# Attention rounds whose scores are formed two units ahead, with the probabilities turned before them

## The chip, the cores and the metric

The kernel runs on one core of a Trainium2 chip. The metric is the device time of one execution in microseconds (us), taken as the median of several runs.

## The reference

Two computations follow one another. Attention over 4 batches of 8 heads, 768 positions and a head size of 64, in which a position sees the 128 positions up to itself and the first four positions ("sinks"), gives a matrix x of 3072 rows and 512 columns. A mixture of eight experts is then applied to x, with gates that are normalized eight times by rows and by columns.

```python
scores = scale * np.matmul(q, k.transpose(0, 1, 3, 2))
keep = is_sink | in_window            # pos < 4, or 0 <= rel < 128
scores = np.where(keep, scores, -1e9)
a = np.exp(scores - np.max(scores, axis=-1, keepdims=True))
a = a / (np.sum(a, axis=-1, keepdims=True) + 1e-09)
x = np.matmul(a, v)                   # turned to 3072 x 512
...
P = np.exp(x @ w_gate - max)          # 8 normalizations by rows and columns
for e in range(8):
    out += P[:, e:e+1] * (np.maximum(x @ w1[e], 0) @ w2[e])
```

## The kernel before

The attention is cut into 48 units, numbered n: a unit is one batch, one block i (0 to 5) of 128 positions and one half of the heads (four heads). For a unit the kernel turns queries and keys (`transpose_qk`, L484 on VectorE or L489 on TensorE), forms the scores of its four heads against up to 260 keys (`scores`, L512), takes each head's maximum on VectorE while it adds the mask (`soften`, L520) and the exponentials with their sums on ScalarE (L523), divides (`divide`: VectorE adds 1e-9 and takes the reciprocal, L529 and L530, and GpSimd scales, L532), turns the probabilities (`transpose_halves`, L569: 16 matmuls of 64 rows each into two banks, which VectorE and ScalarE copy to PT, L571), turns the sinks' probabilities, which GpSimd has gathered into SS (L581, L582), into PS (`transpose_sinks`, L587 and the ScalarE copy L589), and multiplies by the values (`values`, L624). `store_x` takes the result to xr (L641 on ScalarE, L637 on VectorE).

These steps are spread over rounds. In round n before the change stand the scores, maxima, exponentials and division of unit n+1, the turning of unit n and the values of unit n-1. From round 6 on (the steady rounds) the order on every engine is the order in which the code is written, so each engine takes its instructions strictly in that order and waits where one isn't ready. Rounds up to 5 (`early_round`) are ordered by hand on TensorE alone.

TensorE is never left without work: `run_fill` adds to each round a piece of the first expert, which needs one of two things: twelve matmuls into the bank f (L732), whose result ScalarE takes with a relu (L737) and VectorE takes again with a list called `late` (L738), or six matmuls (L748), whose result is added up from a list called `mid` (L756 on VectorE) or on ScalarE. There is one bank f, so a piece waits until the reading of the piece before is over. `late` stands behind the second head's maximum, `mid` behind the last. In some rounds, two blocks at a time, the gates' logits are formed (`run_gates`, L672) in the bank of head 2's scores, and ScalarE copies them (L675); their second transposition (L680) comes in the midst of the fill. Such gate rounds are 9, 15, 19, 23, 27, 31, 35, 39 and 43 (and 47).

PSUM has eight banks here: f, t0 and t1 for turned probabilities, O for the values, and st0 to st3 for the scores of the four heads. Before the change st0 also takes the sinks' transposition of a round. At the end of a round ScalarE has its relu and the casts of weights (L708) or of x (L657) for the experts behind the attention, and GpSimd the subtractions that belong to them (L658, L709).

Behind the attention (from about 225 us) come the gates' normalization and the experts.

Of the kernel before, what the change touches and what calls it, by code (L numbers as in the profile page):

```python
# [11 lines left out]
F32R = mybir.dt.float32r  # L12
# [222 lines left out]
def tile_sink_attention_moe(ctx: ExitStack, tc: tile.TileContext, q, k, v, wg, w1, w2, out):  # L235
# [27 lines left out]
    def f32(ap):  # L263
        return ap.bitcast(F32)
# [105 lines left out]
    def st_tile(shape, k=None):  # L370
        if k is None:
            k, turns[0] = turns[0] % 4, turns[0] + 1
        return ps_st.tile(shape, F32, name=f"st{k}")
# [34 lines left out]
    def flush(todo):  # L408
        for f in todo[:]:
            f()  # L410
        todo.clear()
# [56 lines left out]
                              (k, q)[a][b, h, s * GB * P:(s + 1) * GB * P, c * SQ:(c + 1) * SQ].rearrange("(g t) d -> t g d", t=SQ))  # L468

    def squares_due(n):  # L470
        G, r = divmod(n + 8, 2 * GB)
        if FIRST <= G < 2 * B:
            load_squares(G, PARTS[6 * r:6 * r + 6])

    def transpose_qk(n):

        b, i, hh = units[n]
        us[n] = {}
        h0 = hh * HH
        t = KQ[hh]  # L480
        to = t[:, :, SINK:].rearrange("p r (a c) -> p r a c", a=2)[:, :, :, turn_of(b, i)]
        if n >= 2 * GB * FIRST:
            src = KS[n // (2 * GB)].rearrange("p (r a i t) -> p r a i t", r=HP, a=2, i=GB)[:, hh * NP:(hh + 1) * NP, :, i % GB]
            us[n]["high"] = nc.vector.transpose(to, src).ins  # L484
        else:
            pt = bank2([P, 4, P]) if 2 < n < STEADY + 2 else st_tile([P, 4, P], {0: 0, 1: 3, 2: 0}.get(n, 1))
            for pr in range(NP):
                for j, nm in enumerate(("kr", "qr")):
                    nc.tensor.transpose(pt[:, 2 * pr + j, :], raws[nm, b, i][:, h0 + 2 * pr:h0 + 2 * pr + 2, :].rearrange("p h d -> p (h d)"), ident)  # L489
                    if n < 2 and (pr, j) in ((0, 0), (1, 1)) and (n, pr) != (0, 1):  # L490
                        spin(1, 5 - 2 * pr)
            us[n]["high"] = nc.scalar.copy(to, pt.rearrange("p (r a) t -> p r a t", a=2)).ins
        if i == 1:
            with nullcontext() if steady[0] else tc.issue_after(us[n]["high"]):
                (nc.scalar.copy if steady[0] else nc.vector.tensor_copy)(t[:, :, 0:SINK], t[:, :, place(b, 0)][:, :, 0:SINK])

    def scores(n, pr):

        b, i, hh = units[n]
        u = us[n]  # L500
        K, Q = KQ[hh][:, :, seen(b, i)], KQ[hh][:, :, CW:][:, :, turn_of(b, i)]
        if pr == 0:
            u["sc"] = att.tile([P, HH, CW], F32, name="sc", bufs=3)
            u["st"] = att.tile([P, 3, HH], F32, name="st", bufs=3)
            u["ps"] = {}
        hs = range(2 * pr, 2 * pr + 2)
        ps = {h: st_tile([P, K.shape[2]], h) for h in hs}
        u["ps"].update(ps)

        for h in hs:  # L510
            r0 = (h % 2) * D
            nc.tensor.matmul(ps[h], lhsT=Q[r0:r0 + D, pr, :], rhs=K[r0:r0 + D, pr, :], start=True, stop=True)  # L512

    def soften(n, hs):

        b, i, hh = units[n]
        sc, st, ps = (us[n][x] for x in ("sc", "st", "ps"))
        sc = sc[:, :, seen(b, i)]
        for h in hs:
            us[n]["maxed"] = nc.vector.tensor_tensor_reduce(out=sc[:, h, :], in0=ps[h], in1=masks[place(b, i).start, min(i, 2)][:, seen(b, i)], op0=ALU.add, op1=ALU.min,  # L520
                                           scale=-scale, scalar=3.0e38, accum_out=st[:, 0, h:h + 1]).ins
        for h in hs:
            nc.scalar.activation(sc[:, h, :], sc[:, h, :], AF.Exp, bias=st[:, 0, h:h + 1], scale=-1.0, accum_out=st[:, 1, h:h + 1])  # L523
# [36 lines left out]
    def transpose_halves(n):  # L560

        b, i, hh = units[n]
        sc = us[n]["sc"]
        ws = sorted([(spot(n, 0), 1)] + ([(spot(n - 2, 1), 0)] if i else []))
        ts = [pst.tile([P, len(ws), HH, D], F32, name=f"t{r}") for r in range(2)]
        for h in range(HH):
            for j, (_, w) in enumerate(ws):
                for t, rows in zip(ts, HALF):
                    nc.tensor.transpose(t[:, j, h, :], sc[rows, h, place(b, i + 1 - w)], ident[rows, rows])  # L569
        PT = spots(PTR[hh], [p_ for p_, _ in ws]).rearrange("p h s t -> p s h t")  # L570
        return [lambda: nc.vector.tensor_copy(PT[:, :, :, HALF[0]], ts[0]), lambda: nc.scalar.copy(PT[:, :, :, HALF[1]], ts[1])]  # L571
# [11 lines left out]

    def transpose_sinks(n):

        tsk = st_tile([SK, P], 0 if steady[0] else 3)
        nc.tensor.transpose(tsk, f32(SS[units[n][2]]), ident)  # L587
        PS = us[n]["PS"] = att.tile([SK, P], F32R, name="PS", bufs=4)
        nc.scalar.copy(PS, tsk)  # L589

    def due_keys(n):

# [341 lines left out]
    def steady_round(n):  # L934

        if n % 2 == 0:
            if on(n):
                load_rows(("vr",), n // 2)
            if on(n + 2) and units[n + 2][1] == 0:
                load_sinks(units[n + 2][0])  # L940
        if n in ROWS:
            ROWS[n][0](ROWS[n][1])
        squares_due(n)
        if on(n + 1):
            for pr in range(NP):
                scores(n + 1, pr)
        ending = n >= L - 1
        if ending:
            flush(late)
            flush(mid)  # L950
        if ending:
            run_fill(2)
        lows = transpose_halves(n) if on(n) and not ending else []
        turned = n + 2 < 2 * GB * FIRST
        if on(n + 2) and not turned:
            transpose_qk(n + 2)
        if on(n + 1):
            for h in range(HH):
                soften(n + 1, (h,))
                if h == 1:  # L960
                    flush(late)
        flush(late)
        flush(mid)
        if on(n - 1):
            values(n - 1)
        run_gates(2)
        if on(n + 1):
            for pr in range(NP):
                divide(n + 1, range(2 * pr, 2 * pr + 2))
            if units[n + 1][1]:  # L970
                gather_sinks(n + 1)
        if n == L - 1:
            lows = transpose_halves(n)
        flush(lows)
        flush(coming)
        if on(n) and units[n][1]:
            transpose_sinks(n)
        if turned:
            transpose_qk(n + 2)
        if on(n - 1):  # L980
            store_x(n - 1)
        if n == L:
            gates.extend(later)
            later.clear()
            run_gates(1, True)
        run_fill(1)
        if START + 4 < n < L:
            flush(turned_back)
        run_fill(1)
        flush(turned_back)  # L990
        if n in PIECES:
            in_turn(*plain_tiles(*PIECES[n]), nc.gpsimd if n > 2 * NB else nc.vector)
        if n == L - 8:
            first_pieces.extend(pieces1(0))
        if n == L - 2:
            first_pieces.extend(pieces1(1))
        for _ in range({L - 8: 1, L - 6: 1, L - 4: 1, L - 3: 1, L - 2: 1, L - 1: 1, L: 2}.get(n, 0)):
            in_turn(*first_pieces.pop(0))
        flush(act_end)
        if on(n):  # L1000
            b, i, hh = units[n]
            if (i, hh) == (0, 0):
                spread_sinks(b)
            elif (i, hh) == (0, 1):
                split_sinks(b)
            elif (i, hh) == (1, 0) and b:
                split_sinks_low(b)
        flush(pool_end)
        if L - 10 <= n < L - 2:
            sums1((n - (L - 10)) // 4, (n - (L - 10)) % 4)  # L1010
# [7 lines left out]
            early_round(n)  # L1018
    steady[0] = True
    with tc.manual_schedule():  # L1020
        if units[STEADY][1]:
            gather_sinks(STEADY)
        for n in range(STEADY, L + 1):
            gates += later
            later.clear()
            if n == L - 1:
                bank1 = lambda shape: st_tile(shape, 2 + next(turn[0]) % 2)
                bank2 = lambda shape: st_tile(shape, 1) if next(turn[1]) % 2 == 0 else psf.tile(shape, F32, name="f")
            steady_round(n)
        assert not gates and not later  # L1030
        for todo in (late, mid, coming):
            flush(todo)
        flush(act_end)
        flush(pool_end)
# [241 lines left out]
    def bank2(shape):  # L1276
        tails.append(tails.pop(0))
        return tails[-1][0].tile(shape, F32, name=tails[-1][1])
# [757 lines left out]
```

## Time and profile before

| | |
|---|---|
| runs | 2049.91 us median of 3 (2049.74 to 2049.99) |
| the profiled execution: its own time | 2048.75 us |
| its span, first to last instruction | 2047.0 us |
| granted TensorE clock | 0.999 of full speed |
| TensorE busy | 2030.2 us, 99% of the span |
| VectorE, ScalarE, GpSimd busy | 1500.4, 1330.4, 168.7 us |
| chain that ended last | TensorE 94%, VectorE 2%, ScalarE 2% |

The table is to be read with care: 99% is a mean over 2047 us, of which the rounds that the change touches are the stretch from 34 to 232 us. What the change is worth is read there.

### The profile page before, as it was taken

The page shows a single profiled execution, that of the slowest core. Times are in us where ns is not written, and L with a number is a line of the kernel's source. Part 1 is how long each engine was busy: PE and PEld are TensorE (multiplying, and loading weights), DVE is VectorE, ACT ScalarE, POOL GpSimd, SP SyncE. Part 2 cuts the span into 40 slices and gives each one's busy share as a digit, 9 for nine tenths or more (in the row PEclk, how much of TensorE's full clock was granted, in tenths as well). Part 3 has the DMA queues.
Part 4 walks back from the last instruction along what each step waited for, and adds up shares of the span by engine and source line. Part 5 has one row for each costly group of instructions (what it writes and reads, how often), then busy time and mean ns, then how long its engine had stood idle before and what let it go on. Part 6 is the DMA issues. An engine that isn't in the chain of part 4 may idle for free.

```text
span 2047.0 us, 30434 instructions
## 1 busy us (share of the span) xinstructions
PE 2030.2 (99%) x10305; PEld 1661.1 (81%) x10305; DVE 1500.4 (73%) x2998; ACT 1330.4 (65%) x2727; POOL 168.7 (8%) x397
## 2 busy tenths in 40 slices
PE   9999999999999999999999999999999999999998
PEld 7777877888888888888888888888888888888886
DVE  6888769999999998756668965656655655555556
ACT  7877445778778876465667766656555556556555
POOL 7766400000000000000000000000000000000000
PEclk9999999999999999999999999999999999999999
DMA  8766238778788778777776677767666666666663
GB/s 169 159 120 121 79 108 317 264 279 289 250 293 298 254 261 335 252 225 221 231 236 235 227 248 231 226 207 271 201 203 196 212 196 197 206 196 203 205 190 101
DMA packets 316547, 445.87 MB, mean 218 GB/s; under 512 B 132384, under 2 KB 203488, under 8 KB 314592
## 3 DMA queue, kind: packets, MB, share of 16 engines
q1 hardware_dynamic: 314408, 442.64, 67.9%
q8 instruction: 84, 1.38, 0.3%
q10 hardware_dynamic: 1976, 1.20, 0.2%
q14 instruction: 79, 0.65, 0.1%
HBM read 296.86 MB, written 146.90 MB: 217 GB/s over the span
## 4 chain that ended last, share of the span: by engine, by line
PE 94%; DVE 2%; ACT 2%; issue 1%; DMA 0%; POOL 0%; SPq 0%; DVEq 0%; POOLq 0%; ACTq 0%
PE c L1052 42%; PE o L1766 29%; PE held L1766 12%; PE O L624 2%; PE st L512 2%; PE f L748 1%; PE f L732 1%; ACT sc L523 1%; PE t L569 1%; PE st L732 1%; PE held L1189 0%; POOL sc L532 0%; PE o L1862 0%; DVE acc L1795 0%; PE o L1189 0%
## 5 line engine op out<-in xcount | busy, mean ns | idle before, releaser
L1777 ACT COPY acc<-o 128x512 f32<-128x512 f32 x415 | 243.4, 587 | 404.7 <-PE o L1766 403.8
L1766 PE MATMUL o<-hf,T 128*128 128x512 f32 x1620 | 404.8, 390 | 0.2 <-ACT acc L1780 0.2
L1766 PEld LDWEIGHTS o<-hf,T 128*128 128x128 f32 x1620 | 303.4, 188 | 64.7 <-ACT o L1425 1.5
L1766 PE MATMUL o<-hf,B 128*128 128x512 f32 x1080 | 274.2, 389 | 0.0
L1052 PE MATMUL c<-B,W1a 128*128 128x512 f32 x1068 | 272.2, 390 | 0.4
L1052 PE MATMUL c<-T,W1c 128*128 128x512 f32 x1068 | 256.6, 389 | 0.0
L1425 ACT COPY o<-acc 128x512 f32<-128x512 f32 x416 | 245.8, 591 | 13.0
L1766 PEld LDWEIGHTS o<-hf,B 128*128 128x128 f32 x1080 | 202.5, 188 | 42.0
L1052 PEld LDWEIGHTS c<-B,W1a 128*128 128x128 f32 x1068 | 199.5, 188 | 44.4 <-DVE A12r L1668 2.5
L1052 PEld LDWEIGHTS c<-T,W1c 128*128 128x128 f32 x1068 | 200.5, 188 | 41.7
L1668 DVE SCALAR_TENSOR_TENSOR A11r<-c,PB 128x512 f32<-128x512 f32 x90 | 62.1, 690 | 117.7 <-PE c L1052 116.5
L1672 DVE TENSOR_TENSOR A22r<-c,M 128x512 f32<-128x512 f32 x90 | 62.1, 690 | 115.5 <-PE c L1052 93.7
L1766 PE MATMUL held<-hf,T 128*128 128x512 f32 x540 | 137.1, 389 | 0.0
L1766 PE MATMUL held<-hf,B 128*128 128x512 f32 x540 | 137.0, 390 | 0.0
L1052 PE MATMUL c<-T,W1d 128*128 128x512 f32 x534 | 135.9, 389 | 0.2 <-DVE W1d L1473 0.2
L1052 PE MATMUL c<-T,W1b 128*128 128x512 f32 x534 | 135.7, 389 | 0.0
L1052 PE MATMUL c<-B,W1d 128*128 128x512 f32 x534 | 135.7, 389 | 0.0
L1473 DVE TENSOR_TENSOR hf<-S2r,hf 128x512 fp32r<-128x512 f32 x180 | 119.9, 685 | 3.3 <-ACT hf L1470 3.3
L1766 PEld LDWEIGHTS held<-hf,T 128*128 128x128 f32 x540 | 101.3, 188 | 21.1
L1766 PEld LDWEIGHTS held<-hf,B 128*128 128x128 f32 x540 | 101.1, 188 | 20.8
L1052 PEld LDWEIGHTS c<-T,W1d 128*128 128x128 f32 x534 | 100.1, 188 | 21.3 <-DVE W1d L1473 0.6
L1052 PEld LDWEIGHTS c<-T,W1b 128*128 128x128 f32 x534 | 100.1, 188 | 20.7
(273 smaller groups left out, 3276.5 us busy)
## 6 DMA issues: line engine op xcount, KB each, us to landing
T<-w2s SPq DMA_DIRECT2D x108, 512.0 KB, 4.4
r<-in_moe_w_dram SPq DMA_DIRECT2D x75, 512.0 KB, 6.1
w2s<-T SPq DMA_DIRECT2D x64, 512.0 KB, 3.2
W1a<-w1s SPq DMA_DIRECT2D x56, 512.0 KB, 3.9
W1c<-w1s SPq DMA_DIRECT2D x56, 512.0 KB, 3.7
W1d<-w1s SPq DMA_DIRECT2D x56, 512.0 KB, 3.6
B<-w2s SPq DMA_DIRECT2D x54, 512.0 KB, 4.2
w2s<-B SPq DMA_DIRECT2D x32, 512.0 KB, 4.2
```

Of the source, the lines that this page charges most:

```text
L512: nc.tensor.matmul(ps[h], lhsT=Q[r0:r0 + D, pr, :], rhs=K[r0:r0 + D, pr, :], start=True, stop=True)
L523: nc.scalar.activation(sc[:, h, :], sc[:, h, :], AF.Exp, bias=st[:, 0, h:h + 1], scale=-1.0, accum_out=st[:, 1, h:h + 1])
L569: nc.tensor.transpose(t[:, j, h, :], sc[rows, h, place(b, i + 1 - w)], ident[rows, rows])
L624: nc.tensor.matmul(o_, lhsT=x_, rhs=y_, start=(j < 2), stop=(j >= len(ops) - 2), skip_group_check=True)
L732: nc.tensor.matmul(ps, lhsT=WP[0, u][:, a, kc, c * P:(c + 1) * P], rhs=xchunk(g, w, kc, th), start=(i == 0), stop=(i == 3 * KC - 1))
L1052: nc.tensor.matmul(ps, lhsT=w1(a, k), rhs=x[:, b, k, :], start=(start and j == 0), stop=(stop and j == len(TERMS) - 1), skip_group_check=n ...
L1425: nc.scalar.copy(t, sums[order_of(g)[j]])
L1473: nc.vector.tensor_sub(made_["d"][:, 1], made_["s"], f32(made_["d"][:, 0]))
L1668: return nc.vector.scalar_tensor_tensor(RAW[q, fm], src, 0.0, PBS[part, e, th], op0=ALU.max, op1=ALU.mult)
L1672: nc.vector.tensor_add(w, T[c], T[name])
L1766: nc.tensor.matmul(o, lhsT=W2V[w2_of(q), W2_OF[m]][:, a, k * P:(k + 1) * P], rhs=F[q, H_OF[m]][:, w, :], start=(i == 0 and not late and (b ...
L1777: nc.scalar.copy(sums[m, k], o)
```

## The change

In a steady round n the scores, maxima and exponentials are now those of unit n+2. The division of unit n+1, whose exponentials were made in the round before, stands whole (four heads wide, where it was two pairs) at the round's head. On TensorE the turning of unit n comes first, and the scores behind it. The sinks' probabilities are turned in two halves of 64 rows (`sink_halves`), each into columns 260 to 323 of a bank that the scores of heads 0 and 1 of unit n+2 then fill up to column 259; ScalarE copies each half to PS. The copies of the turned probabilities and of the sinks' halves are written ahead of the maxima. On VectorE the turning of queries and keys, now of unit n+3, comes behind the maxima. Ahead of round 6 the scores, maxima and exponentials of unit 7 and the turning of unit 8 are added, once.

```diff
     def squares_due(n):
-        G, r = divmod(n + 8, 2 * GB)
+        G, r = divmod(n + 9, 2 * GB)
...
-            pt = bank2([P, 4, P]) if 2 < n < STEADY + 2 else st_tile([P, 4, P], {0: 0, 1: 3, 2: 0}.get(n, 1))
+            pt = bank2([P, 4, P]) if 2 < n < STEADY + 3 else st_tile([P, 4, P], {0: 0, 1: 3, 2: 0}.get(n, 1))
...
+    def score_tiles(n, pr):
+
+        us[n].setdefault("banks", {}).update({h: st_tile([P, DM], h) for h in range(2 * pr, 2 * pr + 2)})
...
-        ps = {h: st_tile([P, K.shape[2]], h) for h in hs}
+        ps = {h: u["banks"][h][:, 0:K.shape[2]] for h in hs}
...
+    def sink_halves(n):
+
+        banks = us[n + 2]["banks"] if on(n + 2) else {h: st_tile([P, DM], h) for h in range(2)}
+        ts = [banks[r][0:SK, CW:CW + D] for r in range(2)]
+        for t, rows in zip(ts, HALF):
+            nc.tensor.transpose(t, f32(SS[units[n][2]])[rows, :], ident[rows, rows])
+        PS = us[n]["PS"] = att.tile([SK, P], F32R, name="PS", bufs=4)
+        return [lambda t=t, rows=rows: nc.scalar.copy(PS[:, rows], t) for t, rows in zip(ts, HALF)]
...
         if on(n + 1):
+            divide(n + 1, range(HH))
+        turn_out = transpose_halves(n) if on(n) else []
+        if on(n + 2):
+            score_tiles(n + 2, 0)
+        if on(n) and units[n][1]:
+            turn_out += sink_halves(n)
+        if on(n + 2):
             for pr in range(NP):
-                scores(n + 1, pr)
-        ending = n >= L - 1
-        if ending:
+                scores(n + 2, pr)
+        flush(turn_out)
+        if n >= L - 1:
             flush(late)
             flush(mid)
-        if ending:
             run_fill(2)
-        lows = transpose_halves(n) if on(n) and not ending else []
-        turned = n + 2 < 2 * GB * FIRST
-        if on(n + 2) and not turned:
-            transpose_qk(n + 2)
-        if on(n + 1):
+        turned = n + 3 < 2 * GB * FIRST
+        if on(n + 2):
             for h in range(HH):
-                soften(n + 1, (h,))
+                soften(n + 2, (h,))
                 if h == 1:
                     flush(late)
+        if on(n + 3) and not turned:
+            transpose_qk(n + 3)
         flush(late)
         flush(mid)
         if on(n - 1):
             values(n - 1)
         run_gates(2)
-        if on(n + 1):
-            for pr in range(NP):
-                divide(n + 1, range(2 * pr, 2 * pr + 2))
-            if units[n + 1][1]:
-                gather_sinks(n + 1)
-        if n == L - 1:
-            lows = transpose_halves(n)
-        flush(lows)
         flush(coming)
-        if on(n) and units[n][1]:
-            transpose_sinks(n)
+        if on(n + 1) and units[n + 1][1]:
+            gather_sinks(n + 1)
         if turned:
-            transpose_qk(n + 2)
+            transpose_qk(n + 3)
...
     with tc.manual_schedule():
+        n = STEADY + 1
+        for pr in range(NP):
+            scores(n, pr)
+        transpose_qk(n + 1)
+        for h in range(HH):
+            soften(n, (h,))
```

The lines move by 15 or fewer: L512 becomes L518, L520 L526, L569 L575, L571 L577, L624 L639, L672 L687, L732 L747, L738 L753, L748 L763. The two new ones are L602 (a sink half's transposition) and L604 (its copy).

TensorE, round 27 before (a gate round), from the last of its 16 transpositions on; the four L512 rows stood ahead of these 16, and st with a number is one of the banks st0 to st3:

```order
L512 MATMUL st_2509<-KQ_180 128x260
L512 MATMUL st_2510<-KQ_180 128x260
L512 MATMUL st_2513<-KQ_180 128x260
L512 MATMUL st_2514<-KQ_180 128x260
L569 MATMUL t_2517<-ident,sc 128x64
L569 MATMUL t_2518<-ident,sc 128x64
...
L624 MATMUL O<-PT_188,vr 64x256 x4
L672 MATMUL st_2550<-xr,wg_raw 32x128 x8
L587 MATMUL st_2574<-ident,SS_178 96x128
L748 MATMUL f<-W1f,h_1727 128x512 x3
L680 MATMUL st_2586<-ident,part 128x128 x2
```

TensorE, the same round now:

```order
L575 MATMUL t_2515<-ident,sc 128x64
L602 MATMUL st_2532<-ident,SS_178 96x64
L602 MATMUL st_2533<-ident,SS_178 96x64
L518 MATMUL st_2532<-KQ_184 128x260
L518 MATMUL st_2533<-KQ_184 128x260
L518 MATMUL st_2541<-KQ_184 128x260
L518 MATMUL st_2542<-KQ_184 128x260
L639 MATMUL O<-PT_188,vr 64x256 x4
L687 MATMUL st_2564<-xr,wg_raw 32x128 x8
L763 MATMUL f<-W1f,h_1738 128x512 x3
L695 MATMUL st_2586<-ident,part 128x128 x2
```

The transpositions have moved ahead of the scores, and the sinks' halves stand between them and write into the buffers (2532, 2533) that the scores of heads 0 and 1 write next; the whole transposition L587 behind the gates is gone.

VectorE in that round before, each with the engines whose semaphores it waits for, from the maxima to the first pair of the division:

```order
L520 ISA sc,st<-st_2509,mask_96 128x260 [waits PE_49,Pool_49]
L520 ISA st 128x1
L520 ISA sc,st<-st_2510,mask_96 128x260 [waits PE_49]
L520 ISA st 128x1
L738 SCALAR_TENSOR_TENSOR h_2401<-f,h_2401 128x256 [waits Activation_49]
L520 ISA sc,st<-st_2513,mask_96 128x260 [waits PE_49]
L520 ISA st 128x1
L520 ISA sc,st<-st_2514,mask_96 128x260 [waits PE_49]
L520 ISA st 128x1
L529 TENSOR_SCALAR st<-st 128x2 [waits Activation_49]
L530 RECIPROCAL st<-st 128x2 [waits DVE_49]
```

VectorE in that round now:

```order
L535 TENSOR_SCALAR st<-st 128x4 [waits Activation_49]
L536 RECIPROCAL st<-st 128x4 [waits DVE_49]
L577 COPY PT_189<-t_2514 128x2x4x64 [waits PE_49]
L526 ISA sc,st<-st_2532,mask_96 128x260 [waits Activation_49,Pool_49]
L526 ISA st 128x1
L526 ISA sc,st<-st_2533,mask_96 128x260 [waits Activation_49]
L526 ISA st 128x1
L753 SCALAR_TENSOR_TENSOR h_2402<-f,h_2402 128x256
L526 ISA sc,st<-st_2541,mask_96 128x260 [waits PE_49]
L526 ISA st 128x1
L526 ISA sc,st<-st_2542,mask_96 128x260 [waits PE_49]
```

The division and the copy to PT have moved ahead of the maxima; the maxima of heads 0 and 1 (buffers 2532 and 2533) now wait for ScalarE, where they waited for TensorE.

ScalarE in that round before, from the relu of the round before on, and now:

```order
L737 ACTIVATE h_2401<-f 128x256
L523 ACTIVATE sc,st<-sc,st 128x260 x4
L675 COPY part<-st_2550 128x256
L571 COPY PT_189<-t_2518 128x2x4x64
L589 CAST PS<-st_2574 96x128
L641 COPY xr<-O 128x256 x2
```

```order
L752 ACTIVATE h_2402<-f 128x256
L577 COPY PT_189<-t_2515 128x2x4x64
L604 CAST PS<-st_2532 96x64
L604 CAST PS<-st_2533 96x64
L529 ACTIVATE sc,st<-sc,st 128x260 x4
L690 COPY part<-st_2564 128x256
L656 COPY xr<-O 128x256 x2
```

The copies to PT and PS, now three where they were two, have moved from behind the four exponentials to ahead of them, and read the two buffers that VectorE's first maxima read.

## Rows read from the trace of the kernel before

**Rows 1.** Busy time of each engine over rounds 7 to 45, with clock and DMA share.
```profile
39.36:218.81 179.45, 177.17 (x1850) 135.39 (x1850) 148.41 (x612) 140.18 (x499) 123.06 (x291) 1.00 0.64 129
```

**Rows 2.** Timeline of TensorE in round 20: start, duration, instructions.
```profile
101.48 1.15 PE L512 MATMUL st<-KQ 64*128 64x260 f32 x8
102.46 0.67 PE L569 MATMUL t<-ident,sc 64*128 64x64 f32 x16
103.06 1.08 PE L624 MATMUL O<-PT,vr 128*64 128x256 f32 x8
104.07 0.44 PE L624 MATMUL O<-PS,VS 96*128 96x128 f32 x2
104.35 0.28 PE L587 MATMUL st<-ident,SS 128*96 128x128 f32 x1
104.38 1.65 PE L748 MATMUL f<-W2f,h 128*128 128x512 f32 x6
...
105.97 0.49 PE L512 MATMUL st<-KQ 64*128 64x260 f32 x2
```

**Rows 3.** Waits of TensorE's weight loads in rounds 7 to 45: total, times, longest.
```profile
PEld st L672 <- DVE st L520: 3.8, 9, 0.5
PEld st L512 <- ACT PS L589: 3.6, 9, 0.6
...
PEld st L512 <- ACT xr L641: 2.2, 6, 0.4
...
PEld t L569 <- POOL sc L532: 0.9, 3, 0.4
```

**Rows 4.** Timeline of TensorE in round 27, a gate round.
```profile
131.79 1.15 PE L512 MATMUL st<-KQ 64*128 64x260 f32 x8 [0.36 <-ACT PS L589]
...
134.45 0.65 PE L672 MATMUL st<-xr,wg_raw 128*32 128x128 f32 x16
```

**Rows 5.** Timeline of VectorE there: `late`, head 2's maximum, its accumulator's reading.
```profile
133.63 0.42 DVE L738 SCALAR_TENSOR_TENSOR h<-f,h 128x256 fp32r<-128x256 f32 x1
133.97 0.42 DVE L520 CUSTOM_DVE_ANT_0 sc<-st,mask 128x260 f32<-128x260 f32 x1
134.32 0.08 DVE L520 DVE_READ_ACCUMULATOR2_ANT st<- 128x1 f32 x1
```

**Rows 6.** Timeline of TensorE and ScalarE in round 47, where both were free.
```profile
227.32 0.71 PE L569 MATMUL t<-ident,sc 64*128 64x64 f32 x16
...
228.16 0.59 ACT L571 COPY PT<-t 128x512 f32<-128x512 f32 x1 [0.92 <-PE t L569]
228.64 0.27 ACT L589 CAST PS<-st 96x128 fp32r<-96x128 f32 x1
```

**Rows 7.** Timeline of ScalarE behind round 18's end.
```profile
96.31 0.38 ACT L737 ACTIVATE h<-f 128x256 fp32r<-128x256 f32 x1 [0.19 <-PE f L732]
96.59 0.70 ACT L657 CAST B<-xr 128x256 fp32r<-128x256 f32 x2
97.19 0.62 ACT L708 CAST W2f<-r 128x512 fp32r<-128x512 f32 x1
97.72 0.51 ACT L523 ACTIVATE sc<-sc,st 128x260 f32<-128x260 f32 x1
```

**Rows 8.** Timeline of TensorE and ScalarE in round 6.
```profile
34.55 1.38 PE L512 MATMUL st<-KQ 64*128 64x260 f32 x7
...
37.32 0.60 PE L489 MATMUL st<-ident,kq 128*128 128x128 f32 x4
...
38.72 0.58 ACT L492 COPY KQ<-st 128x512 f32<-128x512 f32 x1
```

**Rows 9.** Timeline of VectorE in round 45: the `mid` addition.
```profile
216.44 0.69 DVE L756 TENSOR_TENSOR acc<-f,acc 128x512 f32<-128x512 f32 x1
```

**Rows 10.** Timeline of TensorE in round 26: its start and its fill.
```profile
127.27 1.15 PE L512 MATMUL st<-KQ 64*128 64x260 f32 x8
...
129.75 0.48 PE L732 MATMUL f<-B,W 128*128 128x256 f32 x2
```

**Rows 11.** Timeline of GpSimd behind round 18's end.
```profile
98.74 1.27 POOL L709 TENSOR_TENSOR W2f<-r,W2f 128x512 fp32r<-128x512 f32 x1
```

More of the change, by code (lines that the diff above doesn't have):

```diff
@@ L500, in scores @@
         u = us[n]
+        if 2 * pr not in u.get("banks", {}):
+            score_tiles(n, pr)
         K, Q = KQ[hh][:, :, seen(b, i)], KQ[hh][:, :, CW:][:, :, turn_of(b, i)]
@@ L584, in transpose_sinks @@
     def transpose_sinks(n):
-        tsk = st_tile([SK, P], 0 if steady[0] else 3)
+        tsk = st_tile([SK, P], 3)
         nc.tensor.transpose(tsk, f32(SS[units[n][2]]), ident)
```

## The prediction

> **What bounds the kernel now.** I began with the rounds as a whole. Over rounds 7 to 45 TensorE is busy for 177.17 of 179.45 us at a full clock, while VectorE has 148.41, ScalarE 140.18 and GpSimd 123.06, and the DMA engines are busy 0.64 of the time [rows 1]. So TensorE sets the pace, and no wait of it is longer than a fraction of a microsecond. Then I read one round without a wait on TensorE's timeline: scores 0.98 us from start to start, the 16 transpositions 0.60, values 1.01 and 0.28, the sinks' transposition 0.03, fill 1.59, and the next round 4.49 behind the first [rows 2]. Such a round is nothing but TensorE's own instructions. Last I read what its weight loads wait for: scores for ScalarE's copies 3.6 and 2.2 us, transpositions for GpSimd's scaling 0.9, and the gates' logits for head 2's maximum 3.8 [rows 3]. The first three can vanish with this change. The fourth is the one to watch: in round 27 head 2's accumulator is read until 134.40 [rows 5] and the logits start at 134.45 [rows 4], so in a gate round VectorE's maxima already end just in time.
>
> **What the change takes away.** The three waits sum to 6.7 us by the weight loader's rows [rows 3], but a weight load may wait beneath a running matmul, and TensorE's drawn idle time in the same stretch is only 2.28 us (179.45 less 177.17) [rows 1]. I take the middle, 4.5, and 0.4 for round 6, which these rows leave out: **-4.9 us**, bounds -2.3 and -7.1. They vanish since scores no longer share a wait with the copies of the round's end, and since the scaling has a whole round instead of the rest of one. VectorE loses 82 two-wide divisions' instructions and gets 41 four-wide ones; it isn't the bound, so I cost that at nothing.
>
> **The new chain.** Call T the start of a round's first transposition. Now the copies to PT and PS stand ahead of the maxima, and the maxima of heads 0 and 1 wait for ScalarE's copies of the sinks' halves, which lie in their banks. Nothing before has that order, so I put it together from round 47, where ScalarE was free. The copy to PT starts 0.84 us behind the first transposition (228.16 less 227.32), the copy to PS 0.48 later, and a 96x128 cast is drawn at 0.27 against 0.59 for 512 columns [rows 6], 0.83 ns for a column, so 0.22 for 64 columns (an estimate). Head 0's maximum may then start at T+0.84+0.48+0.22, with a little for the signal T+1.55. Maxima and `late` follow each other at 0.34 to 0.35 [rows 5]: head 1 at T+1.90, `late` T+2.25, head 2 T+2.59, its accumulator read 0.43 later, T+3.02, and the logits 0.05 behind that, T+3.07. TensorE gets there at T+0.60+0.08 (two halves, below)+0.98+1.01 = T+2.67. So a gate round waits 0.40 us that it did not wait before.
>
> What else ScalarE has at a round's end stands ahead of the copy to PT. The relu begins 0.10 behind the end of the fill and takes 0.28, two casts of x 0.60, a weight's cast 0.53 [rows 4, 7]. With a relu alone it is done before T+0.84.
> Gate rounds: 27 and 39 have the relu alone, 0.40 each; 23, 31, 35 and 43 one cast more (0.10+0.28+0.53 = T+0.91), 0.47 each; 19 has all of it (T+1.51), 1.07; 9 follows a round with a copy of keys as well (0.48 from start to start [rows 7, 8] by the exponentials' spacing), 0.9; 15 in between, 0.5. Together **+5.2 us**. Below: if the copy to PT starts 0.2 sooner in every gate round, 3.4. Above: 8, if piled-up casts delay all of them as in 19.
>
> **The other waits that it adds.**
> - Ahead of round 6: scores of unit 7 (0.98) and four transpositions (0.35) start at 34.55, so that ScalarE copies keys at about 36.2 for 0.48 [rows 8]. It then makes unit 7's four exponentials, 0.50 each [rows 7], to 38.7, and only then copies PT (0.48) and PS, so that head 1's maximum of unit 8 ends near 40.2. Unit 9's keys need the bank st1 at about 38.3, behind transpositions, scores and half-size values. Wait **+2.0**, bounds 1 and 3.
> - Rounds 14, 26 and 38 have values of half the size, so the fill comes early: 2.48 behind the start [rows 10], now 2.56. `late`, which frees f, starts at T+2.25 and takes 0.42 [rows 5]: T+2.67. With the signal 0.2 each, **+0.6**, bounds 0 and 1.
> - Round 45 needs the `mid` addition of 0.69 us [rows 9], behind four maxima: T+2.95 to 3.64, against a fill at 0.98+0.60+1.29+0.08 = T+2.95. **+0.7**.
> - Round 47's fill in st1 waits for ScalarE's copies of the sinks' halves, T+1.75, where TensorE is there at T+0.68: **+1.0**. Nothing else is ahead of it in that round to take the time.
> - GpSimd: each weight subtraction of 1.27 us [rows 11] waits for ScalarE's cast and stands ahead of the next scaling. Where casts pile up (rounds 16 to 19) transpositions may wait for the scaling after all: **+1.0**, bounds 0 and 2.5.
> - TensorE's own work: 36 rounds get two transpositions of 64 rows at 0.04 (0.60 over 16) for one at 0.03 [rows 2], 1.6 us in all. The one of 128 rows stood apart from the others, so that its place may cost more than 0.03. **+0.9**, bounds 0 and 1.6.
>
> **The sum.** 5.2+2.0+0.6+0.7+1.0+1.0+0.9 = 11.4 more and 4.9 less: **+6.5 us**. On the profiled execution's own 2048.75 that is 2055.3; the median of the runs is 1.16 above it, so **2056.4 us**. With every added wait at its lower bound (3.4+1.0+0+0.5+0.8+0+0 = 5.7) and the most taken away the sum is -1.4; with every upper bound (8+3+1+0.9+1.2+2.5+1.6 = 18.2) and the least taken away +15.9.
>
> **Rivals.**
> 1. *Within 0.2%* (4.1 us, about what a measurement of this kernel tells from no change). The same mechanism at smaller waits: copies a little earlier, no pile-up on GpSimd, removed waits worth 6. Sum 5.7+0.9-6 = +0.6 to +4, some 2052. For it speaks that each gate wait hangs on tenths. Chance 0.24.
> 2. *Not slower: the copies don't hold the maxima back.* If head 0's maximum starts by T+1.12 instead of T+1.55, because the copy to PT and the halves' copies are done that much sooner, the logits are never waited for, and `late` and `mid` come in time too: 5.2+0.6+0.7 = 6.5 less, 2049.9 us. Against it: 0.84 of the delay is the copy's start, which in round 47 was not held up by earlier work of ScalarE, since it had idled for 0.92 [rows 6]. Chance 0.08. The Trainium skill, PSUM — Partial Sum Buffer, section Terms, says that two engines may not access a bank and quadrant at once, reads against reads included; by that rule this case can't come from a copy and a maximum that run beside each other in one bank, since they have to follow one another. No row of before shows two such reads, and the sum by the rule is the one above.
> 3. *Faster by over 0.2%.* The weight loader's waits were all real and more hung on them (-7.1 for themselves), and rival 2 holds: 11.4-6.5-7.1 = -2.2, and without the GpSimd, TensorE and half of the prologue terms -5.1, 2044.8 us. Needs several terms at once. Chance 0.07.
> 4. *ScalarE becomes the bound.* Its round now begins with waiting for TensorE (0.84), then 0.48 for PT, 0.35 for PS, 0.4 to the first exponential, 2.04 for four of them and 0.27 for xr: T+4.4 of 4.5, and relu and casts (up to 1.4) behind [rows 2, 6, 7]. If each of the 39 rounds grows by a further 0.2, it is 7.8 more: 2064.2 us. Against it: late exponentials leave a whole round until the division, and ScalarE is idle for a fifth of the stretch [rows 1]. Chance 0.12.
>
> **Chances and range.** The forecast has 0.49, and with rival 4 the side of slower has 0.61; some of the forecast's own spread falls under 4.1 us, so slower 0.62, within 0.2% 0.29 and faster 0.09, with rival 2 counted as the same. The forecast's own range is 2053 to 2060. For 8 in 10 it must take in most of rival 1 and some of rival 4: 2050 to 2063.
>
> **What the changed profile would show.** Right: in the nine gate rounds L687 waits for head 2's maximum L526, 0.4 to 1.1 us each; head 0's maximum starts at about T+1.55, released by ScalarE's L604; in round 6 unit 9's keys (L489) wait some 2 us; in round 45 L747 waits for L771, in round 47 L763 for L604; scores and transpositions wait for ScalarE's copies and GpSimd no more. Wrong: head 0's maximum at T+1.1, or rounds without gates longer than 4.6 us, which is rival 4, or transpositions that wait for the scaling in many rounds. What I see least well is how ScalarE's tail of casts meets the copy to PT.

## The result and the profile after

The changed kernel takes 2060.9 us in the median of 6 runs (2058.97 to 2062.34), against 2049.89 us before, also in the median of 6: a ratio of 1.0053, 95% interval 1.0043 to 1.0064, or 11.0 us more. The forecast was 2056.4 us (2050 to 2063), so direction and range held and the size was short by 4.5 us. The profiled execution has a span of 2058.3 us, 11.3 more than before.

Where the time went is read first from the stretches of rounds. This is the busy time by stretch of the changed kernel, over rounds 7 to 45 (it answers to [rows 1]):

```profile
42.94:230.25 187.31, 177.68 (x1879) 128.85 (x1879) 138.68 (x536) 144.97 (x532) 120.95 (x292) 1.00 0.58 122
```

The stretch has grown by 7.86 us (179.45 to 187.31), but TensorE's busy time by 0.51 only: its idle time has risen from 2.28 to 9.63. So it isn't TensorE's work that got longer. VectorE has 9.7 us less; ScalarE has 4.8 more (144.97 for 140.18), but with 42 us of the stretch idle it isn't full. Round 6 with what now stands ahead of it takes 8.55 us for 4.81, which is 3.74 more (1.3 of it are the scores and the transposition of one more unit, of which the scores are missing again at the end), and the rounds behind 45 take 0.17 more.

What TensorE's matmuls wait for in the attention, from the view of waits of the changed kernel (total, times, longest):

```profile
PE st L687 <- DVE st L526: 7.0, 9, 2.2
PE st L489 <- DVE st L526: 1.9, 1, 1.9
PE f L747 <- DVE h L753: 1.2, 4, 0.7
PE st L763 <- ACT PS L604: 1.0, 1, 1.0
PE f L747 <- DVE acc L771: 0.7, 1, 0.7
PE st L602 <- POOL SS L588: 0.5, 2, 0.3
```

The first five are waits that the prediction named: the gates' logits for the third maximum, unit 9's keys in round 6, late, round 47's fill, mid. The last is GpSimd's, but at another place than forecast: in rounds 18 and 30 the sinks' halves wait until GpSimd has gathered them (L588), where the prediction had the probabilities wait for their scaling. They sum to 12.3 us. The scores' waits for ScalarE [rows 3] are gone.

The chain behind the largest row can be seen in round 27 of the changed kernel, whose first transposition starts at T = 139.21, on TensorE, ScalarE and VectorE:

```profile
139.21 0.71 PE L575 MATMUL t<-ident,sc 64*128 64x64 f32 x16
...
140.84 1.08 PE L639 MATMUL O<-PT,vr 128*64 128x256 f32 x8
142.38 0.64 PE L687 MATMUL st<-xr,wg_raw 128*32 128x128 f32 x16 [0.45 <-DVE st L526]
...
139.99 0.59 ACT L577 COPY PT<-t 128x512 f32<-128x512 f32 x1 [0.29 <-PE st L602]
140.51 0.32 ACT L604 CAST PS<-st 96x64 fp32r<-96x64 f32 x2
141.33 0.51 ACT L529 ACTIVATE sc<-sc,st 128x260 f32<-128x260 f32 x1 [0.50 <-DVE st L526]
...
140.86 0.43 DVE L526 CUSTOM_DVE_ANT_0 sc<-st,mask 128x260 f32<-128x260 f32 x1 [0.21 <-ACT PS L604]
...
142.24 0.08 DVE L526 DVE_READ_ACCUMULATOR2_ANT st<- 128x1 f32 x1
```

The copy to PT starts at T+0.78 (0.84 forecast), the sinks' halves at T+1.30 (1.32), head 0's maximum at T+1.65, released by them (1.55), and the logits at T+3.17 (3.07), 0.5 us behind the place where values end. Round 9 shows the same chain with ScalarE's tail of the round before ahead of it:

```profile
54.18 0.38 ACT L752 ACTIVATE h<-f 128x256 fp32r<-128x256 f32 x1 [0.57 <-PE f L747]
54.46 1.31 ACT L672 CAST B<-xr 128x256 fp32r<-128x256 f32 x4
55.67 0.61 ACT L723 CAST W1f<-r 128x512 fp32r<-128x512 f32 x1
56.19 0.58 ACT L577 COPY PT<-t 128x512 f32<-128x512 f32 x1
...
57.02 0.43 DVE L526 CUSTOM_DVE_ANT_0 sc<-st,mask 128x260 f32<-128x260 f32 x1 [1.51 <-ACT PS L604]
```

The round starts at 54.07, and a relu, four casts of x and a weight's cast hold the copy to PT until T+2.12. VectorE stands idle for 1.51 us ahead of the first maximum, and the logits wait 2.2 us.

### The profile page after: what moved, and what is told of

The parts are those of the page before. It is cut to its first block, busy times and chain, and to the rows that moved or that the text cites. A ratio compares the mean times of both kernels' runs of the same rounds, so it can differ in the third digit from the quotient of the medians.

```text
span 2058.3 us, 30408 instructions
## 1 busy us (share of the span) xinstructions
PE 2032.0 (99%) x10341; PEld 1654.6 (80%) x10341; DVE 1488.5 (72%) x2916; ACT 1336.7 (65%) x2763; POOL 165.1 (8%) x397
## 4 chain that ended last, share of the span: by engine, by line
PE 93%; DVE 3%; ACT 2%; issue 1%; POOL 1%; DMA 0%; SPq 0%; DVEq 0%; ACTq 0%; POOLq 0%
PE c L1070 42%; PE o L1784 29%; PE held L1784 12%; PE O L639 2%; PE f L747 1%; PE f L763 1%; PE st L518 1%; DVE sc L526 1%; PE t L575 1%; PE st L747 1%; PE held L1207 0%; ACT PT L577 0%; POOL sc L538 0%; PE o L1880 0%; PE st L687 0%
```

## The experiments

**The logits in another bank.** They wait for head 2's maximum because they are written to its bank.

```diff
-            lg = st_tile([P, k_, P], 0 if end else 2)
+            lg = st_tile([P, k_, P], 0 if end or steady[0] else 2)
```

> Only edit: in the steady rounds the gates' logits go to head 0's bank instead of head 2's, so that they wait for the first maximum and not for the third. My theory: the maxima are held back by ScalarE's copies of the sinks' halves, and ScalarE's own chain (copies, exponentials, copy of the logits) is as late as theirs. Then the 7.4 us of waits ahead of the logits nearly vanish, but the second transposition of the logits, in the midst of the fill, finds ScalarE's copy of the logits behind the exponentials (ending about T+4.4, with TensorE there at T+4.04) and waits in turn about 0.4 us; only round 9, where that transposition stands behind the fill, keeps its gain of about 1.1. Sum: -1.7 us against the changed kernel, about 2059. Rival (the third maximum is the only trouble): all but 1.0 of the 7.4 us come back, about 2054.5.

Measured: 2058.31 us, ratio to before 1.0042 (1.0026 to 1.0059), 2.6 us less than the changed kernel. From its waits and, below, its timeline in round 27:

```profile
PE st L695 <- ACT part L690: 2.4, 6, 0.7
...
PE st L687 <- DVE st L526: 1.1, 1, 1.1
...
140.45 0.64 PE L687 MATMUL st<-xr,wg_raw 128*32 128x128 f32 x16
...
142.37 0.44 PE L695 MATMUL st<-ident,part 128*128 128x128 f32 x2 [0.38 <-ACT part L690]
```

The logits no longer wait (140.45, right behind the values), and the wait stands two steps further on: their second transposition waits for ScalarE's copy of them, which stands behind the exponentials. So ScalarE is as late as VectorE in a gate round, and a wait at one place doesn't tell what its removal is worth. The time is within 1 us of my theory's 2059; the rival's 2054.5 is out.

**Late ahead of the maxima.** The line `flush(late)` moves to right behind `flush(turn_out)`.

```diff
         flush(turn_out)
+        flush(late)
         if n >= L - 1:
-            flush(late)
             flush(mid)
```

> Only edit: VectorE's late operation stands right behind its copy to PT, ahead of the first maximum, where VectorE waits for ScalarE anyway. My theory: the fills of rounds 14, 26, 38 and their like no longer wait for late (1.3 to 1.5 us back); the logits wait 0.3 us less, but most of that goes to the logits' second transposition, which waits for ScalarE. About -2 us, 2059. Rival (VectorE itself is what is late, so its work ahead of the maxima delays all): the maxima move by a further 0.3 us, exponentials too, no gain or +1 us.

Measured: 2057.94 us, 1.0037 (1.0022 to 1.0051), 3.0 us less, where my theory had 2. The row on late is gone from the waits, and that on the logits has fallen from 7.0 to 4.1 us. VectorE had room ahead of its maxima, so it isn't VectorE's own work that makes them late.

**The halves copied behind the exponentials.**

```diff
...
-            turn_out += sink_halves(n)
+            sink_out = sink_halves(n)
...
         flush(turn_out)
+        if not on(n + 2):
+            flush(sink_out)
...
+        flush(sink_out)
         if on(n + 3) and not turned:
```

> Only edit: ScalarE copies the sinks' halves to PS behind the four exponentials instead of ahead of them, so the first two maxima wait for TensorE and VectorE's own copy alone. My theory: head 0's maximum starts at about T+1.35 instead of T+1.65 in an ordinary round; the logits wait 0.2 us instead of 0.5 in seven gate rounds (-2.1), 0.2 instead of 1.2 in round 19 (-1.0), 0.2 instead of 2.2 in round 9 (-2.0), and the fills behind late lose 0.7: -5.8 us, about 2055. The 2 us of round 6 stay. Rival (VectorE's own copy and the scores behind the transpositions set the maxima): head 0's maximum stays near T+1.6 and the time within 1 us of the changed kernel.

Measured: 2060.68 us, 1.005 (1.0033 to 1.0067): no gain, as the rival has it, but not for its reason. From its waits, and its timeline of TensorE and ScalarE in round 6:

```profile
PE st L489 <- DVE st L535: 3.9, 1, 3.9
PE st L687 <- DVE st L526: 2.4, 9, 0.6
...
PE st L489 <- ACT PS L604: 0.9, 2, 0.5
...
42.89 1.11 PE L489 MATMUL st<-ident,kq 128*128 128x128 f32 x4 [3.91 <-DVE st L535]
43.66 2.91 PE L747 MATMUL f<-B,W 128*128 128x256 f32 x12
...
42.54 0.29 ACT L604 CAST PS<-st 96x64 fp32r<-96x64 f32 x2
```

The logits' row falls to 2.4 us, as my theory has it, and from round 9 to the end of the attention this kernel is 4.6 us shorter than the changed one (184.21 for 188.79). But the keys of units 9, 10 and 11 are turned into the bank st1, and this bank is now held until the copies behind the exponentials: in round 6 TensorE stands for 3.9 us in place of 1.9. (The row names a division, L535. That is the one of the next round, which happens to end with ScalarE's copies at 42.83; in rounds 7 and 8 the same wait is put down to the copies, L604.) And behind that stand its clock is halved: twelve matmuls of the fill take 2.91 us, where the changed kernel's take 1.67. When round 9 starts this kernel is 5.9 us behind the changed one (60.01 for 54.07), which eats up the gain. What I had missed is that a copy holds a bank for others than the maxima.

**The sinks whole, at their old place.**

```diff
-        tsk = st_tile([SK, P], 3)
+        tsk = st_tile([SK, P], 0 if steady[0] else 3)
...
-        if on(n) and units[n][1]:
-            turn_out += sink_halves(n)
...
         flush(coming)
+        if on(n) and units[n][1]:
+            transpose_sinks(n)
```

> Only edit: the sinks' probabilities are turned whole again, at their old place behind the logits into head 0's bank, and copied to PS behind the exponentials; all else of the change stays. My theory: as with the copies moved, -5.5 us, about 2055.4, and scores do not wait for the copy to PS as they did before the change, since 16 transpositions now stand ahead of them. If the two halves cost TensorE more than the whole one, this run is up to 1 us below the one with the copies moved; rival (the whole one is dearer, since it stands alone between others): up to 1.5 us above it.

Measured: 2052.46 us, 1.0012 (1.0002 to 1.0022): 8.4 us less than the changed kernel, by undoing this one part, and 3 us below what I expected. The spans of the two profiled executions differ by less, 5.6 us (2052.7 for 2058.3), since that of this kernel had a halved clock in round 6, which cost it 1.2 us in the fill alone (see the last section). The waits of this kernel:

```profile
PE st L687 <- DVE st L526: 2.4, 9, 0.6
PE st L593 <- DVE st L526: 1.7, 1, 1.7
PE f L747 <- DVE acc L771: 0.3, 1, 0.3
...
```

Beyond the logits (4.6 us less) it has no wait of the sinks' transposition for GpSimd's gathering (0.5) and none of round 47's fill (1.0), which my expectation had left out; those for late and mid have fallen from 1.9 to 0.5, and the scores don't wait for PS. An ordinary round takes 4.47 to 4.51 us with the whole transposition and 4.46 to 4.50 with the two halves, so TensorE's price for either is the same within 0.03.

**The step to two units ahead, later.** Rounds 6 to 11 keep the order of before, and the extra unit ahead of round 6 is gone; in round 11 (CROSS), whose units 12 and 13 have scores of 128 columns, both are formed and softened.

```diff
+        if n <= CROSS:
...
+            if n == CROSS:
+                squares_due(n, 9)
+                for pr in range(NP):
+                    scores(n + 2, pr)
+                for h in range(HH):
+                    soften(n + 2, (h,))
+                transpose_qk(n + 3)
+        else:
...
```

> Edit on the changed kernel: rounds 6 to 10 keep the order of before, the step from one unit ahead to two is made in round 11, whose units 12 and 13 have scores of 128 columns instead of 260 (round 11 forms and softens both), and from round 12 on all is as in the change. My theory: what stands in rounds 6 to 11 of the changed kernel beyond the kernel before is 4.5 us at round 12, of which 1.0 comes back at the end; it is the wait of unit 9's keys in round 6 for the maxima behind the division of unit 7, round 9's logits, and in some executions a TensorE clock that is halved for a few us behind that wait. So -3.5 us in the profile, about -4.5 in the median, 2056.5, and executions that lie within 1.5 us of each other instead of 3.4. Rival (the extra unit's 2 us on ScalarE are lost wherever it is put): only round 9's 2 us come back, 2059, and TensorE waits about 2 us in round 12.

Measured: 2058.4 us, 1.0042 (1.0027 to 1.0057), 2.5 us less: nearer to the rival's 2059 than to my 2056.5. Its 4 runs lie within 0.6 us of each other, where the changed kernel's 6 lie within 3.4.

**The same step, with the sinks whole.**

> The sinks' transposition whole at its old place (the kernel of 2052.46 us) and the step to two units ahead in round 11. My theory: 4.4 us beyond the kernel before at round 12, 1.0 of them returned at the end, go: 2049.1 us, within 1.5 us of the kernel before. Rival (the extra unit costs its 2 us wherever it is put): 2051.

Measured: 2052.68 us, 1.0013 (1.0004 to 1.0022): no gain over the whole sinks alone, and above even the rival's 2051. The rival is right in the main: the step costs about as much in round 11. TensorE's timeline there:

```profile
64.69 0.71 PE L518 MATMUL st<-KQ 64*128 64x128 f32 x8 [0.94 <-ACT PS L595]
...
67.63 1.15 PE L518 MATMUL st<-KQ 64*128 64x260 f32 x8 [0.25 <-ACT KQ L495]
```

The extra scores wait 0.94 us for the copy to PS, since the bank of the sinks' transposition is also that of head 0's scores, and the next round's wait for keys behind the extra exponentials. In the kernel with halves the gain of 2.5 us is about the size of round 9's wait for the logits (2.2), which this order avoids; its row on the logits reads 4.8 us for 7.0.

**Another order in the gate rounds**, with the sinks whole: late behind the last maximum and the last head's exponential behind the copy of the logits; in the other rounds late and mid ahead of the maxima.

```diff
+        gated = len(gates) >= 2 and on(n + 2)
+        if not gated:
+            flush(late)
+            flush(mid)
...
+            for h in range(HH - gated):
                 soften(n + 2, (h,))
...
         run_gates(2)
+        if gated:
+            soften(n + 2, (HH - 1,))
+            flush(late)
+            flush(mid)
```

> The sinks' transposition whole at its old place, and another order of VectorE and ScalarE in the rounds: in a gate round late stands behind the last maximum, and the last head's exponential behind ScalarE's copy of the logits; in the other rounds late and mid stand ahead of the first maximum. Two units ahead from round 6 as in the change. My theory: the logits' waits (3.1 us) fall below 0.6, those for late and mid (1.2) below 0.3, 0.4 us are lost at the logits' second transposition: -3.0 us against 2052.46, 2049.5. Rival (the logits' wait is passed on to the fill or to the next round's division, since ScalarE ends later): -1 us or less, 2051.5.

Measured: 2051.19 us, 1.0005 (0.9996 to 1.0015), 1.3 us less than the whole sinks alone by the medians, so nearer to the rival's 2051.5 than to my 2049.5. From the waits:

```profile
PE st L593 <- DVE st L526: 2.0, 2, 1.7
PE st L687 <- DVE st L526: 0.3, 1, 0.3
```

The logits' row has fallen from 2.4 to 0.3 and the rows on late and mid are gone, as my theory has it, and no row shows that the wait was passed on; what is left is round 6 (1.7) and 0.3 in round 10. A gate round such as 27 takes 5.03 us for 5.35. In the profiled executions TensorE's last group of matmuls starts 5.8 us earlier than with the whole sinks alone (2038.49 for 2044.25; at least 1.2 of it is the other's halved clock), but the span is only 3.8 us shorter. What follows TensorE's last matmuls took 2 us longer; the last section shows where. That can be why the medians show less than half of the 3 us, but for the other runs it isn't shown.

**The sinks whole, this order and the step in round 11, together.**

> All three together: sinks whole, late and mid moved, the step to two units ahead in round 11. My theory: the gains add, 2052.46-3.4-3.0 = 2046.1 us, 0.2% under the kernel before: what is left of the change are the waits that it removes (4 to 5 us) against some 1 us for GpSimd. Rivals: the extra unit costs 2 us anyway, 2048; or the logits' wait is only passed on as well, 2050.

Measured: 2050.91 us, 1.0003 (0.9994 to 1.0012). My 2046.1 is out, and it lies near the second rival's 2050. The gains don't add: as above, the step in round 11 costs about what it costs in round 6.

**The extra scores between the halves of the fill**, in round 11 of that kernel. VectorE's weight subtraction (`coming`) moves too, from ahead of the extra maxima to behind them:

```diff
...
+                run_fill(1)
                 for pr in range(NP):
                     scores(n + 2, pr)
                 for h in range(HH):
                     soften(n + 2, (h,))
+                flush(coming)
                 transpose_qk(n + 3)
```

> Edit on the kernel with sinks whole, late and mid moved and the crossing in round 11: in round 11 the extra scores (unit 13) stand between the two halves of the fill instead of ahead of it, and VectorE's weight subtraction behind the maxima of unit 13 instead of ahead. My theory: the 0.94 us that these scores wait for the copy to PS, which holds head 0's bank, are hidden by half a fill (0.8 us), and the next round's scores wait 0.2 less: -1.0 to -1.3 us against 2050.91, 2049.7, and TensorE's last matmul 0.6 to 0.9 us ahead of the kernel before. Rival (ScalarE's 1.6 us for the extra unit's exponentials are then what is late in round 12): no gain.

Measured: 2050.52 us, 1.0003 (0.9994 to 1.0012), no gain that can be told. Its timeline of TensorE and VectorE in rounds 11 and 12:

```profile
64.50 0.71 PE L518 MATMUL st<-KQ 64*128 64x128 f32 x8 [0.24 <-ACT PS L595]
...
67.44 1.15 PE L518 MATMUL st<-KQ 64*128 64x260 f32 x8 [0.93 <-DVE KQ L484]
...
65.98 0.69 DVE L724 TENSOR_TENSOR W2f<-r,W2f 128x512 fp32r<-128x512 f32 x1
66.59 0.70 DVE L484 STREAM_TRANSPOSE KQ<-W1f 128x512 f32<-128x512 f32 x1
```

The wait for PS falls from 0.93 to 0.24, and the next round's scores wait 0.93 for keys that VectorE turns behind the extra maxima: the wait has moved by a round. The rival has the time right, but what is late is VectorE and not ScalarE's exponentials. And 0.61 of the 0.93 is the weight subtraction (65.98 to 66.59), which this very edit put between the maxima and the keys; what the scores' new place gives without that was not run. So no version here is faster than the kernel before; the last three can't be told from it.

## Why the prediction came out as it did

The mechanism was right: the first maximum behind ScalarE's copies, the logits behind the third, and waits in rounds 6, 45 and 47. Two terms of the sum had the wrong size. By whole parts, undoing the sinks' halves alone gives back 8.4 of the 11.0 us.

Term by term, forecast against the drawn waits of the changed kernel:

- Gates: +5.2 forecast, 7.0 measured. An ordinary gate round was right (0.40 to 0.47 forecast, 0.45 measured in round 27). The step that failed is "what else ScalarE has at a round's end stands ahead of the copy to PT": for round 9 I put a copy of keys and 0.9 us, and it was four casts of x, 1.2 us of them, so the logits waited 2.2. This round alone makes 1.3 of the 1.8 us. The bound of 8 held it, though by its own words (all nine rounds as in 19, 1.07 each) it should have been 9.6.
- Round 6: +2.0, measured 1.9. The place was right, and half of the reason. I had the maxima wait for ScalarE's copies behind unit 7's exponentials. VectorE and ScalarE of the changed kernel show another path:

```profile
39.22 0.17 DVE L535 TENSOR_SCALAR st<-st 128x4 f32<-128x4 f32 x1 [2.26 <-ACT sc L529]
...
40.09 0.42 DVE L526 CUSTOM_DVE_ANT_0 sc<-st,mask 128x260 f32<-128x260 f32 x1
...
39.55 0.31 ACT L604 CAST PS<-st 96x64 fp32r<-96x64 f32 x2
```

  The division (L535) at the round's head waits for unit 7's exponentials, VectorE's copy and the first maximum follow it without a gap, and ScalarE's copies are over at 39.86, before that maximum. The kernel with whole sinks still has 1.7 us there. So here it is the whole division at the head, together with the extra unit, and not the sinks' halves.
- Late: +0.6, measured 1.2. Rounds 14, 26 and 38 wait 0.17 each where I put 0.2, and round 10, which I had not listed, 0.66: it has half-size values and scores of 128 columns, so its fill comes earlier still. Mid +0.7, measured 0.7; round 47 +1.0, measured 1.0; GpSimd +1.0, drawn 0.5 in rounds 18 and 30 (against the kernel with the whole sinks these two rounds are 0.65 and 0.41 longer, 5.59 for 4.94 and 4.92 for 4.51).
- TensorE's own work: +0.9, measured 0.5 busy over rounds 7 to 45. An ordinary round is no longer than before (4.46 to 4.50 us for 4.49 to 4.51), so where the 0.5 lies isn't shown.
- What the change takes away: -4.9, and this is the second step that failed, "I take the middle" between the weight loads' rows and TensorE's drawn idle time. The kernel of 2050.91 us has the waits of before gone and hardly one added behind round 12; from the start of round 14 to the start of the last values it takes 156.30 us (74.62 to 230.92) for 158.66 before (72.59 to 231.25), and about 1.0 of this difference is one unit's scores that were formed earlier. So the removed waits are worth about 1.4 us there. With the 0.96 us that TensorE idled before in rounds 7 to 13 that is 2.3 (an estimate): the lower bound, and not 4.9. Most of the 6.7 us that weight loads waited lay beneath running matmuls.

The two steps make up 1.8 and 2.6 us, late 0.6, GpSimd and TensorE's own work -0.9: with them the sum of 6.5 becomes 10.6. Against that, TensorE reaches the last values 11.6 us later (242.86 for 231.25), so about 1 us is not accounted for; that the span has grown by 11.3 comes of a further 0.8 behind the attention and 1.1 less behind TensorE's last matmuls. That the forecast's range held is due to its width, since both terms erred to the same side.

Of the rivals, 1 (within 0.2%) and 3 (faster) are out by the time. The one in which ScalarE becomes the bound is out: ordinary rounds without a gate take 4.46 to 4.50 us, and the longer ones (4.92 in round 30) have a wait of their own. That the copies don't hold the maxima back is out by round 27's rows. The Trainium skill, PSUM — Partial Sum Buffer, section Terms, has it that two engines may not be on one bank and quadrant at once, even to read; the trace agrees in so far as round 27's first maximum starts at 140.86, behind the casts out of its bank and the next (140.51 to 140.83), and no run here lets the two overlap.

What stays open is why the last three kernels, whose TensorE is done with the attention at about the time of before, end 0.4 to 1.1 us later in the median. The end of the last section shows where the profiled executions of two of them lose it, not why.

## What to carry to other kernels

Before an operation is put ahead of others in an engine's queue, list what stands ahead of it in that queue at each kind of round (here ScalarE's casts for another stage), for the longest list set the highest price here (2.2 us in round 9). A bank that two uses share ties their engines to each other; the tie and the order that came with it, not TensorE's work, were 8 of 11 us here by the medians. And a deeper lookahead has to be paid for once: the extra unit's work cost about the same at both places where it was tried, rounds 6 and 11.

## What the runs showed of the hardware

TensorE's granted clock fell to half, from 2.4 to 1.2 GHz, behind the stand in round 6 in three of the six profiled kernels that have this stand. The busy time by stretch of the kernel with whole sinks, whose TensorE had stood for 1.68 us until 41.02 (the clock is the third column from the end, behind the engines):

```profile
40.00:42.00 2.00, 0.98 (x6) 0.85 (x7) 1.92 (x9) 1.10 (x6) 1.86 (x4) 0.91 0.62 96
42.00:44.00 2.00, 2.00 (x11) 2.00 (x11) 0.35 (x2) 1.90 (x8) 0.97 (x4) 0.50 0.61 97
44.00:46.00 2.00, 2.00 (x26) 1.71 (x26) 0.48 (x1) 1.29 (x3) 1.91 (x7) 0.74 0.72 145
```

The fill behind it takes 2.91 us in place of 1.67. The clock also fell with late ahead of the maxima (a stand of 1.9 us) and with the halves copied late (3.9). It stayed at 1.00 in the changed kernel (1.94), with the logits in another bank (1.9) and with the other order in the gate rounds (1.7). So stands of the same length went either way. That this is why the changed kernel's runs spread over 3.4 us is a guess: only profiled executions show a clock by stretch, and the spreads don't part the kernels cleanly (1.5 to 3.4 us with the stand, 0.6 to 1.9 with the step in round 11, 0.9 to 2.3 for the kernel before).

The time from TensorE's last matmuls to the end isn't fixed. In the kernel of 2050.91 us the last row of TensorE is the first of these; the others are SyncE's issue of an output transfer, there and in the kernel before:

```profile
2038.44 1.04 PE L1934 MATMUL held<-ident,acc 128*128 128x128 f32 x8
2040.57 2.25 SPq L1922 DMA_DIRECT2D out_dram<-ro  x1
...
2040.04 0.51 SPq L1870 DMA_DIRECT2D out_dram<-ro  x1
```

The matmuls start 0.37 us later than the same row before (2038.07), but the span ends at 2049.4, 2.4 us later. The same issue takes 2.25 us in place of 0.51, so the last transfer is issued at 2043.63 in place of 2041.33. The kernel of 2051.19 us has 2.23 there. From the start of that last row of TensorE to the end it is 7.8 us in the changed kernel, 8.4 with the whole sinks, about 9 before and 10.4 to 10.9 in the last three kernels. Why an issue takes longer no run here tells.
